# Maxima over partitions by a matmul with the identity instead of POOL's partition operation, with the schedule made anew

## The chip, the cores and the metric

The kernel runs on one core of one Trainium2 chip. Its engines work side by side, each through its own instructions in order: PE multiplies matrices (TensorE) and writes to PSUM; DVE (VectorE), ACT (ScalarE) and POOL (GpSimd) work on elements; SP (SyncE) issues all transfers between memory and the core. The metric is the time of one execution in microseconds, as the device counts it. Its median before the change is 1002.06 us of three runs.

## The reference

Linear attention with random features, and a feed-forward layer over its output.

```python
def phi(x):                                   # x: q or k, scaled by 64 ** -0.25
    proj = np.einsum('bhsd,md->bhsm', x, omega)
    sq = np.sum(x * x, axis=-1, keepdims=True) / 2.0
    h = proj - sq
    h = h - np.max(h, axis=-1, keepdims=True)
    return np.exp(h) / np.sqrt(m)
kv = np.einsum('bhsm,bhsd->bhmd', k_p, v)
z = np.sum(k_p, axis=2)
num = np.einsum('bhsm,bhmd->bhsd', q_p, kv)
den = np.einsum('bhsm,bhm->bhs', q_p, z)[..., None] + 1e-06
x = (num / den)                               # laid out as 4608 tokens x 512
h = x @ w_in                                  # 512 x 2048
out = np.maximum(0.01 * h, h) @ w_out         # 2048 x 512
```

There are 8 batches of 576 tokens, 8 heads of 64, and 128 features. The weights come as 64-bit numbers, which the kernel reads as pairs of 32-bit words. Everything else is float32.

## The kernel before

**Numbers.** Large products are made with pairs of 16-bit numbers, a high part and the rest (`high` and `low_` in the code; three matmuls for each product). To keep the parts in range, omega, the values of each batch and both weights are scaled by a power of two that comes from their largest magnitude. That largest magnitude is first a maximum per partition (`mx_om`, `mx_v0` to `mx_v7`, `mx_w1`, `mx_w2`: eleven in all) and then a maximum over the 128 partitions. The second step is `power_of_two`, at L315 to L330: POOL's `partition_all_reduce` (L320) leaves the maximum in every partition, and four small DVE steps (L324 to L328) cut it to its exponent and invert it. What waits for them: the split of omega, the scaling of the values (`values`), the scaling of a weight's pieces (`Weight.split`), the rows of scales for the output (L644).

**Tiling.** The feed-forward layer works on nine blocks of 512 tokens. For each block, 16 groups of 12 matmuls (L813) make the hidden layer, ACT applies the leaky step (L820), ACT and POOL split it into two parts (L290, L296), and 16 groups of 12 matmuls (L836) make the output. Attention is made ahead of it, batch by batch for keys (`key_batch`) and block by block for queries (`query_block`), two heads at a time. A unit (`Unit`) loads its rows, takes squares, scales (L490 to L495), makes two parts (L506 or L290 and L296), turns them by a transposing transfer (L508), projects them (L520), and has DVE and ACT make the features (L526 to L537). The first two key batches and the first query block are done in whole float32 (`Whole`, L580 to L590), without those transfers. Sums for keys are L682 and L694 to L696, for queries L758 to L765. Both write 260 columns of one PSUM bank of 512, called "mi", of which there is one.

**Weights.** Each weight comes as eight pieces of 1 MB. A piece is converted (`convert`): ACT takes the high words (L403), DVE shifts and joins the low words (L405, L408), PE sums magnitudes (L416), and the sign is put on in one of two ways: by DVE in one step (L426), or, for pieces named in `SIGN_POOL`, by ACT (L421) and POOL (L423). When all eight are done, the maximum of the sums gives the scale (`scale`), and each piece is scaled and split, in one of two ways chosen by `SPLIT_DVE` (L450 or two ACT steps and L296). `Z_POOL` makes the like choice for the units of the first batches or blocks: a unit below its number is scaled in an ACT step of its own and then split.

**Order.** The instructions of each engine stand in an order that a planner in the file works out beforehand (`Plan.order`). Every step has a cost, the buffers it reads and writes, a priority, and sometimes a slack. The planner gives each free engine the step that is ready by its own times. While feed-forward groups are there to fill PE, a step with a slack counts as ready only `SLACK["PE"]` times that slack later; projections and sums of attention have a slack of 1. `PACE` and `LATER` shift the priorities of weights, keys and queries. `PRICE` weighs an engine's time where a step may go to either of two: `high` to ACT or DVE, `low_` to POOL or DVE. The step at L320 is entered as POOL, 0.6 us, the small steps behind it as DVE, 0.65 us. Transfers stand in SP's own order.

The functions that the diff touches, and what calls them:

Of the kernel before, what the change touches and what calls it, by code (L numbers as in the profile page):

```python
# [13 lines left out]
ALU = mybir.AluOpType  # L14
AX = mybir.AxisListType
PSUM = bass.MemoryType.PSUM

P = 128
# [9 lines left out]


EXP_SHIFT = 10.375  # L30
SIGN_POOL = {"w1": [0, 1, 2, 3, 7], "w2": [2]}
SPLIT_DVE = {"w1": [0, 1, 2, 3, 4, 5], "w2": [0, 1, 4, 5, 7]}
Z_POOL = {"k": 1, "q": 2}
PACE = {"k": 9.5, "q": 9.5, "w1": 10.0, "w1s": 0, "w2": 12.0, "w2s": 22.5}

WHOLE = 2
SLACK = {"PE": 1.5}
LATER = {"w1": 20.0, "w2": -295.0, "k": 15.0, "q": -40.0}
ONE = 2.0 ** 14
KV_DOWN = 2.0 ** -24  # L40
H_DOWN = 2.0 ** -15
# [21 lines left out]
class Plan:  # L63
# [2 lines left out]

    HOP = {"PE": 0.25, "ACT": 0.08, "DVE": 0.08, "POOL": 0.10}

    PRICE = {"PE": 1.0, "ACT": 0.68, "DVE": 17.64, "POOL": 1.0, "SP": 1.0}

    def __init__(self, places):
        self.places, self.ops = places, []
# [39 lines left out]
    def order(self):  # L112
# [40 lines left out]
        while len(done) < len(self.ops):  # L153
# [4 lines left out]
            for o in sorted(open_, key=lambda o: (o.prio, o.number)):  # L158
# [3 lines left out]
                if filler:  # L162
                    t += SLACK["PE"] * o.slack
                e = min(o.ways, key=lambda e: max(free[e] + load[e], t) + self.PRICE[e] * o.ways[e][0])
                if t < free[e] + load[e] + 2.0:
# [52 lines left out]
def act(n, pointers=0):  # L218
    return 0.19 + n / 1190 + 0.09 * pointers
# [19 lines left out]
def performer_ffn(ctx: ExitStack, tc, qT, kT, qn, kn, vn, omT, eye, w_in, w_out, out):  # L239
    nc = tc.nc  # L240
# [28 lines left out]
    tiles = {k: [sb.tile(shape, dt, tag=f"{k}{i}", name=f"{k}_{i}") for i in range(n)]  # L269
             for k, (n, shape, dt) in kinds.items()}  # L270
    for k, (n, size) in banks.items():
        tiles[k] = [ps.tile([P, size], F32, tag=f"{k}{i}", name=f"{k}_{i}") for i in range(n)]
    plan = Plan({k: len(v) for k, v in tiles.items()})
    buf, ways = plan.buf, plan.op

    def op(engine, cost, run, port=False, **of):
        return ways([(engine, cost, run, port or engine == "POOL")], **of)

    def high(n, dst, src, scale=None, psum=False, **of):

        pointer = scale is not None and not isinstance(scale, float)
        value = (lambda: scale()) if pointer else (lambda: scale)

        def dve_run():
            if scale is None:
                nc.vector.tensor_copy(dst(), src())
            else:
                nc.vector.tensor_scalar(dst(), src(), value(), None, op0=ALU.mult)
        return ways([
            ("ACT", act(n, int(pointer)), lambda: nc.scalar.activation(dst(), src(), AF.Copy,  # L290
             scale=1.0 if scale is None else value()), False),
            ("DVE", dve(n) if psum else dve2(n), dve_run, not psum)], **of)
# [6 lines left out]
    def at(b):  # L299
        return tiles[b.kind][b.place]  # L300
# [11 lines left out]
    ident = one("ident", [P, P])  # L312


    def power_of_two(mx, name, prio):  # L315


        t = one(f"pow_{name}", [P, 4])
        key = f"pow_{name}"
        op("POOL", 0.6, lambda: nc.gpsimd.partition_all_reduce(t[:, 2:3], mx, P,  # L320
           reduce_op=bass.bass_isa.ReduceOp.absmax), r=[f"mx_{name}"], w=[key], prio=prio)

        def run():
            nc.vector.tensor_scalar(t[:, 1:2].bitcast(U32), t[:, 2:3].bitcast(U32), 0x7F800000, None,  # L324
                                    op0=ALU.bitwise_and)
            nc.vector.tensor_scalar(t[:, 1:2], t[:, 1:2], 2.0 ** -100, None, op0=ALU.max)
            nc.vector.reciprocal(t[:, 3:4], t[:, 1:2])
            nc.vector.tensor_scalar(t[:, 0:1], t[:, 3:4], ONE, None, op0=ALU.mult)  # L328
        op("DVE", 0.65, run, r=[key], w=[key], prio=prio)
        return t, key  # L330


# [4 lines left out]
    def omega():  # L337
        mx = one("mx_om", [P, 1])
        op("SP", 0.45, lambda: nc.sync.dma_start(out=om32(), in_=omT), w=[(whole, "om")], moved=131072, prio=-0.9)
        op("SP", 0.45, lambda: nc.sync.dma_start(out=ident, in_=eye), w=["ident"], moved=65536)  # L340

        def constants():
            nc.vector.memset(ones, 1.0)
            nc.vector.memset(shift, EXP_SHIFT)
            nc.vector.memset(minus_half(), 0.0)
            for j in range(2):
                nc.vector.memset(minus_half()[64 * j:64 * j + 64, j * M:(j + 1) * M], -0.5 * QK_SCALE ** 2)
        op("DVE", 1.0, constants, w=["ones", (whole, "half")], prio=-0.9)

        def scaled():  # L350
            nc.vector.tensor_scalar(om32(), om32(), QK_SCALE, None, op0=ALU.mult)
            nc.vector.tensor_reduce(mx, om32(), axis=AX.X, op=ALU.max, apply_absolute_value=True)
        op("DVE", 0.8, scaled, w=[(whole, "om"), "mx_om"], prio=-0.9)
        t, key = power_of_two(mx, "om", 0)

        def split():
            nc.vector.tensor_scalar(om_c, t[:, 1:2], OM_DOWN, None, op0=ALU.mult)
            for j in range(2):
                r = slice(64 * j, 64 * j + 64)
                a = om32()[r, j * M:(j + 1) * M]  # L360
                nc.vector.tensor_scalar(om[r, 0, :], a, t[r, 0:1], None, op0=ALU.mult)
                nc.vector.scalar_tensor_tensor(om[r, 1, :], a, t[r, 0:1], om[r, 0, :], op0=ALU.mult,
                                               op1=ALU.subtract)
        op("DVE", 1.3, split, r=[(whole, "om"), key], w=["om", "om_c"], prio=0.005)


    class Weight:
# [26 lines left out]
        def convert(self, i, prio):  # L394
# [17 lines left out]
            def sums():  # L412
# [6 lines left out]
               slack=6.0)  # L419
            if i in SIGN_POOL[self.name]:  # L420
                op("ACT", act(1130), lambda: nc.scalar.activation(at(f), high().bitcast(F32), AF.Sign), r=[b], w=[f],  # L421
# [7 lines left out]
        def scale(self, prio):  # L429
            mx = one(f"mx_{self.name}", [P, 1])  # L430

            def run():

                sums = at(self.sums)[:, self.col0:self.col0 + 64]
                if self.name == "w1":
                    nc.vector.tensor_reduce(self.mxs, sums.rearrange("p (f k) -> p f k", k=4), axis=AX.X, op=ALU.add)
                    nc.vector.tensor_reduce(mx, self.mxs, axis=AX.X, op=ALU.max)
                else:
                    nc.vector.tensor_reduce(mx, sums, axis=AX.X, op=ALU.max)
            op("DVE", 0.4, run, r=[(self.sums, self.name, i) for i in range(8)], w=[f"mx_{self.name}"], prio=prio)  # L440
            self.pow, self.key = power_of_two(mx, self.name, prio)

        def split(self, i, prio):
# [3 lines left out]
            whole = lambda: at(f)  # L447
            if i in SPLIT_DVE[self.name]:
                high(1024, lambda: part(0), whole, lambda: self.pow[:, 0:1], r=[f, self.key], w=[(t, 0)], prio=prio)
# [7 lines left out]
        def part(self, i, j):  # L457
            return at(self.parts[i]).bitcast(F16).rearrange("p (a b) -> p a b", a=2)[:, j]
# [5 lines left out]
    class Unit:  # L464
# [7 lines left out]
        def prepare(self):  # L472
# [26 lines left out]
            zh, zl = lambda: at(z)[:, :2 * nt, :D], lambda: at(z)[:, :2 * nt, D:]  # L499
            if self.i < Z_POOL[self.what]:  # L500
                high(n, heads, heads, up, r=[self.sc], w=[nat], prio=prio)
# [104 lines left out]
    def values(b, prio):  # L606
# [9 lines left out]
        for j in range(2):  # L616
# [3 lines left out]
        op("DVE", 0.17, lambda: nc.vector.tensor_reduce(mx, mx2, axis=AX.X, op=ALU.max),  # L620
           r=[f"mx2_v{b}0", f"mx2_v{b}1"], w=[f"mx_v{b}"], prio=prio)
        t, key = power_of_two(mx, f"v{b}", prio)
        hi = lambda: at(both).bitcast(F16)[:, :, :].rearrange("p a b -> p (a b)")[:, :HP * VT * 2 * E].rearrange(
            "p (g d) -> p g d", d=E)
# [28 lines left out]
    def key_batch(b, prio):  # L653
# [6 lines left out]
        for hp in range(HP):  # L660
            plan.like("k", PACE["k"])
            if b >= WHOLE:
# [55 lines left out]
    def query_block(j, prio):  # L718

        for hp in range(HP):  # L720
            plan.like("q", PACE["q"])
            u = Unit("q", j, hp, prio) if j else Whole("q", j, hp, prio)
# [69 lines left out]
    def in_turn(*of):  # L792

        for _ in zip(*of):
            pass
# [51 lines left out]


    omega()
    wsums = buf("ffn")  # L850
    w1, w2 = Weight(w_in, "w1"), Weight(w_out, "w2")
    in_turn(key_batch(0, 1e-4 * LATER["k"]), query_block(0, 1e-4 * LATER["q"]))
    for w in (w1, w2):
        for i in range(8):
            plan.like(w.name, PACE[w.name])
            w.load(i, 1e-4 * LATER[w.name])
            w.convert(i, 1e-4 * LATER[w.name])
        plan.like()
        w.scale(1e-4 * LATER[w.name])
        for i in range(8):  # L860
            plan.like(w.name + "s", PACE[w.name + "s"])
            w.split(i, 1e-4 * LATER[w.name])
    plan.like()
# [61 lines left out]
```

## Time and profile before

| what | value |
|---|---|
| median of three runs | 1002.06 us (1000.24 to 1005.46) |
| the profiled execution | 999.61 us |
| its span (first to last instruction) | 997.8 us |
| busy: PE, DVE, ACT, POOL | 948.5, 561.5, 518.3, 251.3 us |
| granted clock of PE over the span | 0.979 |
| feed-forward matmuls (L813 and L836) | 383.6 and 384.3 us |
| maxima over partitions (L320) | 11, of 0.41 us each |

The profile shows one execution on the chip. "Busy" counts the time in which an engine worked on data, not the time it waited. "Idle before" a group of instructions is what the engine stood still ahead of them, with what released it behind an arrow; "issue" is time in which the engine waited for nothing that the profile shows. The chain of waits goes back from the last instruction, at each step to what released it.

### The profile page before, as it was taken

The numbers are of one execution on the slowest core, as the hardware profiler recorded it, in microseconds if no ns is written. First come the engines' busy times: TensorE is split into PE (matmuls) and PEld (weight loads), VectorE is DVE, ScalarE is ACT, GpSimd is POOL, SyncE is SP. The second block draws the span as 40 slices with busy tenths as digits, with TensorE's granted clock in tenths as the row PEclk, the third lists the DMA queues.
The fourth block names the chain that finished last, engine by engine and source line by source line (L and its number), as shares of the span: only waits on it lengthen the run. The fifth ranks groups of instructions, "written<-read, shape, count | busy, mean of one in ns | idle before, by whom it ended". The sixth has DMA issues, their size and how long they took to land.

```text
span 997.8 us, 16453 instructions
## 1 busy us (share of the span) xinstructions
PE 948.5 (95%) x6576; PEld 523.3 (52%) x6576; DVE 561.5 (56%) x1103; ACT 518.3 (52%) x738; POOL 251.3 (25%) x247
## 2 busy tenths in 40 slices
PE   3778899899899999999999999999999999999998
PEld 3667655555455555555555555554444444444443
DVE  5597966887888887887888888872110000000000
ACT  4368455856584585666775685566114303402410
POOL 2130233300440253112510441024104302401410
PEclk9799799899999999999999999999999999999999
DMA  9463724366356782675585555660430110000000
GB/s 369 143 214 96 215 60 91 74 165 125 66 107 159 131 160 69 141 160 108 102 175 133 99 107 119 129 115 1 74 75 1 32 32 22 1 22 22 1 8 35
DMA packets 211821, 98.69 MB, mean 99 GB/s; under 512 B 170016, under 2 KB 200480, under 8 KB 210720
## 3 DMA queue, kind: packets, MB, share of 16 engines
q1 hardware_dynamic: 211744, 97.64, 42.4%
q8 instruction: 51, 0.84, 0.4%
q14 instruction: 26, 0.21, 0.1%
HBM read 46.50 MB, written 9.44 MB: 56 GB/s over the span
## 4 chain that ended last, share of the span: by engine, by line
PE 78%; DVE 13%; issue 5%; ACT 2%; DMA 1%; POOL 1%; SPq 0%; DVEq 0%; ACTq 0%
PE ffn L836 34%; PE ffn L813 31%; PE pj L520 4%; PE mi L682 3%; DVE st L526 1%; DVE wt L408 1%; DVE p L534 1%; DVE st L586 1%; PE pj L581 1%; PE pj L580 1%; DVE ph L296 1%; PE mi L758 1%; DVE ph L588 1%; DVE wt L405 1%; PE mi L760 1%
## 5 line engine op out<-in xcount | busy, mean ns | idle before, releaser
L836 PE MATMUL ffn<-wt,big 128*128 128x512 f16 x1728 | 384.3, 380 | 0.0
L813 PE MATMUL ffn<-xt,wt 128*128 128x512 f16 x1728 | 383.6, 380 | 0.0
L813 PEld LDWEIGHTS <-wt 128*128 128x128 f16 x1728 | 166.5, 98 | 193.2 <-issue 1.7
L836 PEld LDWEIGHTS <-big 128*128 128x128 f16 x1728 | 166.1, 98 | 191.8 <-issue 1.4
L296 POOL TENSOR_TENSOR big<-row,big 128x512 f16<-128x512 f32 x144 | 177.0, 1233 | 338.5 <-ACT big L290 291.3
L820 ACT ACTIVATE row<-ffn 128x512 f32<-128x512 f32 x144 | 85.2, 592 | 131.9 <-PE ffn L813 79.1
L296 POOL TENSOR_TENSOR xn<-x,xn 128x512 f16<-128x512 f32 x36 | 44.7, 1242 | 231.0 <-ACT xn L290 148.1
L290 ACT ACTIVATE row<-ffn,s 128x512 f32<-128x512 f32 x36 | 24.6, 684 | 147.3 <-PE ffn L836 147.1
L537 ACT ACTIVATE p<-p,shift 128x1024 f32<-128x1024 f32 x68 | 69.8, 1029 | 47.5 <-DVE p L534 47.4
L290 ACT ACTIVATE big<-row 128x512 f16<-128x512 f32 x144 | 90.1, 626 | 2.8
L526 DVE TENSOR_REDUCE st<-pj 128x8 f32<-128x1024 f32 x68 | 72.4, 1075 | 10.8 <-PE pj L520 10.7
L296 DVE TENSOR_TENSOR ph<-p,ph 128x1024 f16<-128x1024 f32 x56 | 70.5, 1261 | 13.4 <-ACT ph L290 13.0
L534 DVE SCALAR_TENSOR_TENSOR p<-pj,sc,st 128x1024 f32<-128x1024 f32 x68 | 76.4, 1132 | 0.3
L778 DVE TENSOR_TENSOR x<-mi,r 128x256 f32<-128x256 f32 x72 | 30.1, 419 | 63.4 <-POOL xn L296 62.3
L520 PE MATMUL pj<-om,t 128*128 128x128 f16 x944 | 61.7, 219 | 3.8 <-DVE p L534 3.0
L520 PEld LDWEIGHTS <-t 128*128 128x128 f16 x944 | 55.0, 98 | 10.3 <-issue 3.4
L290 ACT ACTIVATE ph<-p 128x1024 f16<-128x1024 f32 x56 | 58.7, 1048 | 0.6
L483 ACT ACTIVATE z<-nat 128x512 f32<-128x512 f32 (+1 forms) x56 | 36.0, 645 | 25.6 <-DMA t<-z 13.4
L506 DVE SCALAR_TENSOR_TENSOR z<-nat,sc,z 128x512 f16<-128x512 f32 (+1 forms) x52 | 45.9, 886 | 4.3 <-ACT z L290 4.1
L775 DVE TENSOR_SCALAR r<-mi 128x4 f32<-128x4 f32 x72 | 11.3, 157 | 62.1 <-PE mi L760 61.9
L290 ACT ACTIVATE z<-nat,sc 128x512 f16<-128x512 f32 (+1 forms) x52 | 38.0, 737 | 12.9 <-DVE sc L493 12.9
L290 ACT ACTIVATE xn<-x 128x512 f16<-128x512 f32 x36 | 22.4, 623 | 42.5 <-DVE x L778 36.3
(107 smaller groups left out, 1010.2 us busy)
## 6 DMA issues: line engine op xcount, KB each, us to landing
v<-vn SPq DMA_DIRECT2D x16, 650.0 KB, 5.7
out<-row SPq DMA_DIRECT2D x36, 256.0 KB, 2.1
big<-w_in SPq DMA_DIRECT2D x8, 1024.0 KB, 7.5
big<-w_out SPq DMA_DIRECT2D x8, 1024.0 KB, 5.3
nat<-qn SPq DMA_DIRECT2D x32, 256.0 KB, 3.2
nat<-kn SPq DMA_DIRECT2D x12, 320.0 KB, 3.5
nat<-kn SPq DMA_DIRECT2D x12, 256.0 KB, 3.4
nat<-kT SPq DMA_DIRECT2D x4, 320.0 KB, 5.6
```

The lines of the kernel that those rows point to most:

```text
L290: ("ACT", act(n, int(pointer)), lambda: nc.scalar.activation(dst(), src(), AF.Copy, scale=1.0 if scale is None else value()), False),
L296: return ways([(e, c, lambda g=g: g.tensor_tensor(dst(), a(), b(), op=ALU.subtract), True) for e, c, g in (("POOL", pool_(n), nc.gpsimd), ...
L483: op("ACT", act(n), lambda: nc.scalar.activation(square(), flat(at(nat)[:, :nt, :]), AF.Square, scale=SQ_SCALE), r=[nat], w=[z], prio=prio)
L506: op("DVE", stt(n) + 0.15, lambda: nc.vector.scalar_tensor_tensor(zl(), heads(), up(), zh(), op0=ALU.mult, op1=ALU.subtract), port=True, r ...
L520: nc.tensor.matmul(pv()[:, g], at(self.t)[:, g0 + g, :], om[:, w, :], start=(w == 0), stop=(w == 1))
L526: op("DVE", dve(n * M), lambda: nc.vector.tensor_reduce(row(0), pv(), axis=AX.X, op=ALU.max), r=[pj], w=[st], prio=prio)
L534: op("DVE", dve(n * M), lambda: nc.vector.scalar_tensor_tensor(p(), pv(), down(), row(2).rearrange("p (g o) -> p g o", o=1).broadcast_to([ ...
L537: op("ACT", act(n * M, 1), lambda: nc.scalar.activation(flat(p()), flat(p()), AF.Exp, bias=shift), w=[p32], r=["ones"], prio=prio)
L778: op("DVE", dve(4 * D), lambda av=av, r=r, x=x, i=i: nc.vector.tensor_tensor(at(x)[:, i * 256:(i + 1) * 256].rearrange("p (g d) -> p g d", ...
L813: nc.tensor.matmul(at(ph), wk[wp][:, c:c + P], xt[:, xp, :], start=(i == 0), stop=(i == 3 * KT - 1))
L820: op("ACT", act(512), lambda ph=ph, g=g: nc.scalar.activation(at(g), at(ph), AF.Prelu, scale=H_DOWN, alpha=0.01), r=[ph], w=[g], prio=top)
L836: nc.tensor.matmul(at(po), part(f, gp)[:, t * P:(t + 1) * P], wf[wp], start=(f == 0 and gp == wp), stop=(f == FT - 1 and gp == 1))
```

## The change

The maximum over partitions goes to PE and DVE. The column of 128 maxima, repeated 128 times, is the stationary operand of a float32 matmul, and the identity matrix the moving one: row after row, the result holds all 128 maxima in each partition. It is written to the last 128 columns of the "mi" bank. DVE takes the maximum of each row, and the four small steps follow as before, in the same entry. The identity's load gets the priority of omega's. The numbers that steer the planner are others: which pieces have their sign put on by POOL (seven of w1 instead of five, four of w2 instead of one), which are split in DVE's one-step way (five of w1 instead of six, seven of w2 instead of five), for which units the input is scaled by itself (keys below 3, queries below 3), the paces, priorities, slack and prices.

```diff
-SIGN_POOL = {"w1": [0, 1, 2, 3, 7], "w2": [2]}
-SPLIT_DVE = {"w1": [0, 1, 2, 3, 4, 5], "w2": [0, 1, 4, 5, 7]}
-Z_POOL = {"k": 1, "q": 2}
-PACE = {"k": 9.5, "q": 9.5, "w1": 10.0, "w1s": 0, "w2": 12.0, "w2s": 22.5}
+SIGN_POOL = {"w1": [0, 1, 2, 3, 4, 5, 7], "w2": [0, 1, 2, 7]}
+SPLIT_DVE = {"w1": [0, 1, 4, 6, 7], "w2": [0, 1, 2, 4, 5, 6, 7]}
+Z_POOL = {"k": 3, "q": 3}
+PACE = {"k": 13.5, "q": 9.5, "w1": 0, "w1s": 4.0, "w2": 5.5, "w2s": 15.0}
...
-SLACK = {"PE": 1.5}
-LATER = {"w1": 20.0, "w2": -295.0, "k": 15.0, "q": -40.0}
+SLACK = {"PE": 0.5}
+LATER = {"w1": 0.0, "w2": -305.0, "k": -25.0, "q": -570.0}
...
-    PRICE = {"PE": 1.0, "ACT": 0.68, "DVE": 17.64, "POOL": 1.0, "SP": 1.0}
+    PRICE = {"PE": 1.0, "ACT": 1.09, "DVE": 12.14, "POOL": 1.0, "SP": 1.0}
...
+    scratch = tiles["mi"][0][:, 384:]
...
-        op("POOL", 0.6, lambda: nc.gpsimd.partition_all_reduce(t[:, 2:3], mx, P,
-           reduce_op=bass.bass_isa.ReduceOp.absmax), r=[f"mx_{name}"], w=[key], prio=prio)
+        op("PE", 0.35, lambda: nc.tensor.matmul(scratch, mx.broadcast_to([P, P]), ident, start=True, stop=True),
+           r=[f"mx_{name}", "ident"], w=["scratch"], prio=prio, slack=1.0)
 
         def run():
+            nc.vector.tensor_reduce(t[:, 2:3], scratch, axis=AX.X, op=ALU.max)
...
-        op("DVE", 0.65, run, r=[key], w=[key], prio=prio)
+        op("DVE", 0.95, run, r=["scratch"], w=[key], prio=prio)
...
-        op("SP", 0.45, lambda: nc.sync.dma_start(out=ident, in_=eye), w=["ident"], moved=65536)
+        op("SP", 0.45, lambda: nc.sync.dma_start(out=ident, in_=eye), w=["ident"], moved=65536, prio=-0.9)
```

## The prediction

> **What bounds the kernel now.** I read the page's totals first, then the busy time by stretches.
>
> ```profile
> span 997.8 us, 16453 instructions
> PE 948.5 (95%) x6576; PEld 523.3 (52%) x6576; DVE 561.5 (56%) x1103; ACT 518.3 (52%) x738; POOL 251.3 (25%) x247
> ...
> 0.00:120.00 120.00, 83.39 (x491) 72.85 (x492) 89.40 (x140) 67.77 (x82) 26.17 (x28) 0.86 0.65 213
> 120.00:200.00 80.00, 75.58 (x492) 43.15 (x491) 59.04 (x100) 51.65 (x71) 25.32 (x26) 0.95 0.37 75
> 200.00:365.00 165.00, 162.40 (x1386) 89.87 (x1385) 138.87 (x287) 105.22 (x152) 41.76 (x45) 1.00 0.63 128
> 365.00:440.00 75.00, 73.09 (x608) 40.34 (x606) 62.77 (x133) 46.70 (x69) 19.09 (x20) 1.00 0.54 118
> 440.00:680.00 240.00, 240.00 (x2058) 133.19 (x2057) 202.53 (x416) 161.60 (x231) 65.75 (x65) 1.00 0.59 121
> 680.00:997.80 317.80, 314.04 (x1553) 143.87 (x1551) 8.89 (x31) 85.33 (x137) 73.16 (x63) 1.00 0.10 25
> ```
>
> In the stretches the columns after the length are busy time of PE, its weight loads, DVE, ACT and POOL, the granted clock, the DMA share and GB/s. PE is idle for 997.8 - 948.5 = 49.3 us: 36.61 before 120 us, 4.42 to 200, 2.60 to 365, 1.91 to 440, none to 680, and 3.76 at the end, where the last block is evicted and stored. The matmuls stay the same but for eleven small ones. So time can only come out of these gaps, or out of the stretch in which the clock is 0.86.
>
> The chain of waits names what makes the gaps (start, length, what):
>
> ```profile
> 3.76 5.06 issue
> 8.81 0.42 POOL pow_om L320
> ...
> 24.92 6.23 issue
> ...
> 46.42 1.93 issue
> ...
> 74.64 3.54 issue
> ...
> 133.30 3.43 issue
> ...
> 168.56 5.70 issue
> ...
> 246.44 1.38 issue
> ...
> 384.20 4.29 issue
> ```
>
> Each of these eight pieces stands right before a POOL L320, as the first does. That operation runs 0.42 us; what precedes it is a code load of POOL:
>
> ```profile
> L320 POOLq MODIFY_POOL_CONFIG  x22: 1/11/15, 1.0 to 531.7; - x22
> ...
> 255.57 2.28 POOL L296 TENSOR_TENSOR big<-row,big 128x512 f16<-128x512 f32 x2 [7.34 <-DVE r L776]
> ...
> DVE pow_v L324 <- POOL pow_v L320: 23.6, 6, 6.7
> DVE pow_w L324 <- POOL pow_w L320: 10.1, 2, 6.1
> DVE pow_om L324 <- POOL pow_om L320: 5.5, 1, 5.5
> ```
>
> There are 22 configuration changes for 11 reductions: one into the reduction and one back, after which the next ordinary POOL work waits again (7.34 us at 255.57). DVE, which works in order, stands for 23.6 + 10.1 + 5.5 = 39.2 us at L324. The written order charges 0.6 us for the operation, so much that is ready lies behind that wait: maxima of projections, their subtraction, the splitting of weights.
>
> **The change, part by part.** The maximum itself. Removed from the chain: 5.06 + 6.23 + 1.93 + 3.54 = 16.76 us before 120, 9.13 before 200 and 5.67 later, with 0.42 for each reduction. Added, eleven times: one fp32 matmul of the identity and one DVE maximum over 128 values. The nearest rows:
>
> ```profile
> L739 PE MATMUL ffn<-ident,ph 128*128 128x128 f32 x32 | 5.1, 311 | 1.2 <-ACT ph L590 1.2
> L739 PEld LDWEIGHTS ffn<-ident,ph 128*128 128x128 f32 x32 | 4.4, 169 | 1.4 <-ACT ph L590 1.4
> L436 DVE TENSOR_REDUCE mxs_w<-ffn 128x16 f32<-128x64 f32 x1 | 0.2, 216 | 0.0
> L352 DVE TENSOR_REDUCE mx_om<-xt 128x1 f32<-128x256 f32 x1 | 0.4, 421 | 0.0
> ```
>
> Weight load 0.17 + matmul 0.31 + a reduction between 0.22 and 0.42 (0.29 in proportion) + two hand-overs, which I estimate together at 0.13: 0.9 us, where the chain had 0.42 and the code load. Upper bound: the matmul falls behind a group of 12 FFN matmuls (2.59 us by the two busy rows, 380 ns each being pipelined ones), giving 3.5. Lower bound 0.77, no hand-over. I take 0.9 in the startup, where no FFN group runs.
>
> Startup: 16.76 + 4 x 0.42 - 4 x 0.9 = 14.8 us. Of the omega piece (5.06) I count half, since at that time the first inputs are still arriving and the next DVE work may be late instead: 12.3. Bounds: 0, if everything else is as late, and 14.8.
>
> 120 to 200: the chain would give 9.13 + 0.84 - 1.8 = 8.2, but PE has FFN work to fill with and only 4.42 us of gaps: I take 3.5 (0 to 4.42). 200 to 440: the chain would give 1.38 + 4.29 + 0.84 - 1.8 = 4.7, the gaps are 4.51. DVE is busy 62.77 of 75 us at 365 to 440, and its other work may be late next: I take 2 (0 to 4.5). The last DVE waits fall where PE has no gap, and give nothing.
>
> Cost on PE: seven of the eleven matmuls fall where PE is full. Each takes between its pipelined share (5.1/32 = 0.16) and 0.48: 0.3, so 2 us. Bounds 1 and, if PE stands at each until the maximum is there, 7 x 3.5 = 24 (the longest such waits below).
>
> The clock. The same kind of work at two places of the chain, and the first FFN matmuls behind it:
>
> ```profile
> 87.42 2.32 PE mi L682 x20
> ...
> 110.53 8.79 PE mi L682 x40
> 119.32 11.61 PE ffn L813 x48
> ```
>
> Forty sums took 8.79 us at 110.53 where 2 x 2.32 = 4.64 is the better rate: 4.15 lost there, after a stretch with gaps. All that the clock can give is 83.39 x 0.14 + 75.58 x 0.05 = 15.5 us; none at the other end. With fewer gaps I take 5, near the one place that shows a price. The Trainium skill, "TensorE: Matmul & The Clock Gate" (Part 1), says that PE drops to half its clock after an idle window of about 3.4 us and needs as long a busy one to come back. By that rule the two long gaps alone would matter and the term would be about 6; the rows above agree with half speed, none shows the threshold.
>
> Signs on POOL: two more pieces of w1 and three of w2 lose the DVE step L426 and take an ACT and a POOL step instead.
>
> ```profile
> L426 DVE SCALAR_TENSOR_TENSOR wt<-wt,wt 128x1024 uint32<-128x1024 uint32 x10 | 12.1, 1216 | 0.0
> L421 ACT ACTIVATE wt<-big 128x1024 f32<-128x1024 f32 x6 | 6.9, 1148 | 7.6 <-DVE wt L405 7.6
> 33.96 1.22 DVE L408 SCALAR_TENSOR_TENSOR wt<-big,wt 128x1024 uint32<-128x1024 uint32 x1
> 40.13 3.27 DVE L408 SCALAR_TENSOR_TENSOR wt<-big,wt 128x1024 uint32<-128x1024 uint32 x1
> 39.49 2.84 POOL L423 TENSOR_TENSOR wt<-wt,wt 128x1024 f32<-128x1024 f32 x1 [6.82 <-ACT edge L590]
> ```
>
> DVE saves 5 x 1.22 = 6.1, but L408 took 3.27 instead of 1.22 while POOL's L423 ran: 5 x 2.05 = 10.3 is lost if each meets such a step. Between -6.1 and +4.2 I take nothing; half of the meetings would cancel it. ACT's 5 x 1.15 = 5.7 hides in its 120 - 67.77 = 52 idle us; without that cover they would stand in the weights' path.
>
> The rest, in its order in the diff.
>
> ```profile
> L290 ACT ACTIVATE nat<-nat,sc 128x512 f32<-128x512 f32 x4 | 2.9, 714 | 4.2 <-DVE sc L493 4.2
> ...
> 13.41 0.37 PE L416 MATMUL ffn<-ones,wt 128*128 128x1 bf16 x8 [13.41 <-DVE wt L408]
> ```
>
> Eight more units scale their input in a step of ACT by itself (0.71, so 5.7 us of ACT, hidden in the same way; at worst all of it in the units' path). One weight piece more is split in DVE's one-step way, a step of DVE for a step of DVE; the identity's load moves to the head of SP's queue, ahead of the weights, 64 KB at the 213 GB/s of that stretch being 0.3 us, plus one issue of 0.45; DVE's lower price can move steps there only where ACT or POOL is far behind. Together: 0, between -1 and +7.
>
> The order made anew has no row. PE's first matmul comes at 13.41 us; if that wait stays, 36.61 - 13.41 = 23.2 us of the startup's gaps are the most that any order can close, 10.9 more than the 12.3 counted. It can also open new ones (second rival). I take 0 for it beside the terms above.
>
> Sum: 12.3 + 3.5 + 2 + 5 - 2 = 20.8; the profiled execution took 999.61 us (span 997.8 and 1.8 around it), so 978.8, rounded 979. That execution lies just under the lowest of the runs shown (1000.24; their median is 1002.06). I don't shift for that; it is inside the range.
>
> **The rivals.** (1) Something else is late in the startup. DVE is busy for 89.40 of 120 us, and the weights, the whole of block 0 and its attention go through it. For it: two of the four startup pieces are already short. Against: the other two aren't covered by anything. Then half of the startup and half of the clock's gain: 12.3/2 + 3.5 + 5/2 - 2 = 10.2, 989.
>
> (2) Slower: PE waits in the middle. The slack that the order leaves ahead of projections and attention sums falls from 1.5 to 0.5 us. PE works in order, so whatever is later than planned then stops the FFN matmuls behind it.
>
> ```profile
> L526 DVE TENSOR_REDUCE st<-pj 128x8 f32<-128x1024 f32 x68 | 72.4, 1075 | 10.8 <-PE pj L520 10.7
> L775 DVE TENSOR_SCALAR r<-mi 128x4 f32<-128x4 f32 x72 | 11.3, 157 | 62.1 <-PE mi L760 61.9
> ...
> PE mi L765 <- DVE x L778: 8.5, 3, 3.8
> PE mi L682 <- DVE x L778: 6.6, 3, 3.5
> ```
>
> There are 68 + 72 = 140 such steps beside the key sums. The point where it decides: a mean wait of 20.8/140 = 0.15 us. At 0.25 us each it costs 35, so 979 + 35 = 1014. For it: a margin that falls by 1.0 us. Against: PE has no gap at all from 440 to 680, and an FFN group of 2.59 us rounds most starts up.
>
> (3) No change: the maximum's matmul writes columns 384 to 511 of the one "mi" bank, which the attention sums use. If accesses to the bank are put in turn, each of the eleven waits for a reader of the sums, and the next sums wait for the maximum. PE's waits for that bank's reader average (8.5 + 6.6)/6 = 2.5 us; 11 x 2.5 = 28 is lost if every one meets a reader, 979 + 28 = 1007; a few will find the bank free, and I take 1003. The Trainium skill, "PSUM — Partial Sum Buffer" (PSUM bank collisions raise a hardware error), asks that accesses of two engines be kept apart by bank and not by address. It speaks against this place; no run here shows the wait yet.
>
> (4) The new order goes further: the clock's 15.5 in place of 5, and the 10.9 us more of the startup's gaps, 979 - 10.5 - 10.9 = 958. For it: DVE is idle for 30.6 of the first 120 us. Against: the first inputs have to be there.
>
> That the change doesn't do what it says, code loads that remain, I give no chance of its own: L320 is the only line with configuration changes, and it goes.
>
> **How the numbers follow.** Forecast 0.60, rival (1) 0.12, (2) 0.10, (3) 0.07, (4) 0.11. The range 960 to 1000 leaves out (2), half of (3) and some of (4), 0.18 together. No change means within 0.5%, 997 to 1007, about what a measurement of this kernel can tell: 0.07; faster is the forecast with (1) and (4), 0.83; slower 0.10.
>
> **What would show it.** Right: no L320 configuration changes; DVE's first step after each maximum within 1.5 us; no "issue" of over 2 us ahead of one; the first FFN matmul at about 119 - 12.3 - 4 = 103 us; PE idle of about 30 us in all; the last DVE-heavy stretch ending some 20 us sooner. Clock over 0.90 in the first 100 us bears out the clock's term. Wrong: PE waits between 200 and 680 that add up to over 10 us (rival 2), PE waits at the new matmul for a reader of "mi" (rival 3), or a startup that has kept its length with other waits in it (rival 1).

## The result, and the profile after

The changed kernel takes 972.81 us (median of four runs, 966.78 to 975.21), the kernel before 1003.22 us beside it (1000.24 to 1005.46). The ratio is 0.969, with a 95% interval of 0.9638 to 0.9742. The forecast was 979 us, within 960 to 1000. The profiled executions are 999.61 us before and 966.78 after, so the terms of the forecast, which add up to 20.8 us, stand against 32.8 us there. Both executions are the shortest of those measured beside them; by the medians the gain is 30.4 us.

The profile page's totals of the changed kernel, and its busy time by the stretches that the prediction showed for the kernel before (PE, weight loads, DVE, ACT, POOL, granted clock, DMA share, GB/s):

```profile
span 965.0 us, 16453 instructions
PE 943.4 (98%) x6598; PEld 520.4 (54%) x6598; DVE 559.9 (58%) x1110; ACT 528.4 (55%) x749; POOL 264.7 (27%) x241
...
0.00:120.00 120.00, 103.01 (x620) 78.34 (x621) 108.57 (x155) 84.86 (x106) 44.62 (x31) 0.90 0.70 225
120.00:200.00 80.00, 80.00 (x607) 48.97 (x607) 63.61 (x136) 58.67 (x78) 21.46 (x24) 1.00 0.47 106
200.00:365.00 165.00, 165.00 (x1421) 92.41 (x1418) 139.22 (x289) 116.10 (x171) 53.77 (x53) 1.00 0.59 125
365.00:440.00 75.00, 75.00 (x637) 42.06 (x636) 63.02 (x148) 46.45 (x66) 16.39 (x22) 1.00 0.62 134
440.00:680.00 240.00, 240.00 (x1954) 130.41 (x1953) 179.68 (x363) 150.42 (x215) 68.61 (x61) 1.00 0.54 108
680.00:965.00 285.00, 280.39 (x1371) 128.22 (x1369) 5.81 (x23) 71.87 (x116) 59.90 (x52) 1.00 0.08 23
```

PE has no gap any more from 120 to 680 us, where it had 8.93 us. Before 120 us it is idle for 16.99 instead of 36.61 us, and DVE is busy for 108.57 instead of 89.40. The gaps fall from 49.3 to 21.6 us, and PE's busy time falls by 5.1 although there are 22 more matmul records.

The first feed-forward matmul of the changed kernel, a piece of its chain of waits, and PE's waits over the whole span:

```profile
88.59 2.10 PE L816 MATMUL ffn<-xt,wt 128*128 128x512 f16 x9
...
89.42 4.69 DMA xt<-xn
94.11 0.04 issue
94.15 4.85 PE ffn L816 x15
...
PE mi L322 <- DVE mx_om L355: 3.7, 1, 3.7
PE ffn L816 <- DMA xt<-xn: 3.5, 1, 3.5
PE mi L768 <- DVE x L781: 3.0, 4, 1.4
```

The first feed-forward matmul comes at 88.6 us and not at 119.1. Nine are done, then PE waits 3.5 us for a transfer of turned tokens and goes on at 94.15. L322 is the new matmul. It waits 3.7 us once, for omega at the very start, where PE has nothing else, and practically nowhere later.

The groups of the new operations, and the first weight's maximum in order of time, on DVE and PE:

```profile
L322 PE MATMUL mi<-ident,mx_v 128*128 128x128 f32 x16 | 3.4, 297 | 0.5 <-DVE mx_v L623 0.5
L326 DVE TENSOR_REDUCE pow_v<-mi 128x1 f32<-128x128 f32 x8 | 2.2, 280 | 0.3 <-PE mi L322 0.3
...
51.53 0.17 DVE L440 TENSOR_REDUCE mx_w<-mxs_w 128x1 f32<-128x16 f32 x1
52.36 0.44 PE L322 MATMUL mi<-ident,mx_w 128*128 128x128 f32 x2
53.13 0.26 DVE L326 TENSOR_REDUCE pow_w<-mi 128x1 f32<-128x128 f32 x1
```

The maximum costs DVE 0.28 us and PE 0.43 us (3.4 us over eight; two records each). From the column of maxima (51.70) to DVE's reduction (53.13) it is 1.43 us, of which DVE spends part on other work, and PE the start on attention sums. For the second weight it is 2.6 us (123.67 to 126.28). The old path had 3.5 us of "issue" at this place alone.

### The profile page after: what moved, and what is told of

The parts are those of the page before. It is cut to its first block, busy times and chain, and to the rows that moved or that the text cites. A ratio compares the mean times of both kernels' runs of the same rounds, so it can differ in the third digit from the quotient of the medians.

```text
span 965.0 us, 16453 instructions
## 1 busy us (share of the span) xinstructions
PE 943.4 (98%) x6598; PEld 520.4 (54%) x6598; DVE 559.9 (58%) x1110; ACT 528.4 (55%) x749; POOL 264.7 (27%) x241
## 4 chain that ended last, share of the span: by engine, by line
PE 91%; DVE 5%; DMA 2%; issue 1%; SPq 0%; POOL 0%; ACT 0%; POOLq 0%; ACTq 0%
PE ffn L839 39%; PE ffn L816 39%; PE pj L523 5%; DMA v<-vn 2%; DVE wt L411 1%; PE mi L761 1%; PE mi L685 1%; PE mi L762 1%; PE mi L763 1%; PE mi L697 1%; PE mi L699 1%; DVE wt L408 1%; PE mi L698 1%; DVE ph L591 1%; PE pj L583 1%; DVE st L589 1%
## 5 line engine op out<-in xcount | busy, mean ns | idle before, releaser
L297 POOL TENSOR_TENSOR big<-row,big 128x512 f16<-128x512 f32 x144 | 182.3, 1267 | 365.2 <-ACT big L291 361.7
L297 DVE TENSOR_TENSOR ph<-p,ph 128x1024 f16<-128x1024 f32 x56 | 73.0, 1308 | 10.8 <-ACT ph L291 10.6
L488 DVE TENSOR_REDUCE sq<-z 128x8 f32<-128x512 f32 (+1 forms) x56 | 39.1, 702 | 6.3 <-ACT z L486 6.2
L291 ACT ACTIVATE z<-nat,sc 128x512 f16<-128x512 f32 (+1 forms) x43 | 31.3, 733 | 19.0 <-DVE sc L496 19.0
```

The costliest lines, as they stand in the source:

```text
L297: return ways([(e, c, lambda g=g: g.tensor_tensor(dst(), a(), b(), op=ALU.subtract), True) for e, c, g in (("POOL", pool_(n), nc.gpsimd), ...
L488: op("DVE", dve(n), lambda: nc.vector.tensor_reduce(at(self.sq)[:, :2 * nt], square().rearrange("p (g d) -> p g d", d=D), axis=AX.X, op=AL ...
```

## Experiments

**The exchange alone, in the old order.** The kernel before, with every engine's order kept as it was: where POOL's reduction stood, the matmul and DVE's maximum are issued. The identity's transfer moves up to right behind omega's.

```diff
-        op("POOL", 0.6, lambda: nc.gpsimd.partition_all_reduce(t[:, 2:3], mx, P, ...
+        op("POOL", 0.6, lambda: nc.tensor.matmul(scratch, mx.broadcast_to([P, P]), ident, start=True, stop=True),
...
+            nc.vector.tensor_reduce(t[:, 2:3], scratch, axis=AX.X, op=ALU.max)
```

> The kernel before with the exchange alone, every engine's order left as it was: in place of each POOL reduction stand the matmul and DVE's maximum at the same place of the order, and the identity is loaded right behind omega. Theory A (the code loads on the chain are most of the gain): the terms of the prediction without the new order, 999.6 - 21, so 975 to 985, first feed-forward matmul at about 103 us instead of 119. Theory B (the order made anew carries the gain, other work is late in the old one): 990 to 1000, startup nearly as long, with DVE waits at other lines.

Measured: 969.23 us, ratio 0.967 (0.9647 to 0.9693). Theory A holds, and the gain is larger than it said. The first feed-forward matmul comes at 101.74 us. The order made anew isn't needed for the gain. DVE still waits for the maximum in this order, for the matmul now, but for 12.6 us in all and at most 2.5 us at once, where it was 39.2.

**The exchange with the planner's old numbers.** Here the order is planned anew for the new operation, with the numbers of before.

```diff
-SLACK = {"PE": 0.5}
+SLACK = {"PE": 1.5}
... (and SIGN_POOL, SPLIT_DVE, Z_POOL, PACE, LATER, PRICE as before)
```

> The changed kernel with all the planner's numbers of before (where signs and splits go, paces, priorities, slack, prices): the exchange, with an order planned anew for it, but not with the new numbers. Theory A: 975 to 985, since planning with a true price adds a few us at most to the exchange. Theory B: 985 to 1000, and only the new numbers bring the rest of the way to 973.

Measured: 987.4 us, ratio 0.9841 (0.9813 to 0.9868). Theory A's number is missed: an order planned with the new operation's own price and engine didn't add to the exchange, it lost 18 us of it. PE's busy row of the first stretch in this kernel, and its longest wait:

```profile
0.00:120.00 120.00, 82.36 (x516) 69.03 (x517) 104.16 (x163) 71.25 (x85) 22.42 (x20) 0.87 0.63 219
...
PE ffn L419 <- DVE wt L411: 17.4, 7, 5.9
```

The loss is all in the startup: PE is idle for 37.6 of 120 us there, 17.4 of them for DVE's conversion of weights, and full from 120 to 440 us. With the old numbers, planning anew gives a worse order than the old one kept as it was.

**POOL's reduction in the new order.** The changed kernel, each engine's order kept, with POOL's reduction at the place of each matmul.

```diff
-        op("PE", 0.35, lambda: nc.tensor.matmul(scratch, mx.broadcast_to([P, P]), ident, start=True, stop=True),
+        op("PE", 0.35, lambda: nc.gpsimd.partition_all_reduce(t[:, 2:3], mx, P, ...
...
-            nc.vector.tensor_reduce(t[:, 2:3], scratch, axis=AX.X, op=ALU.max)
```

> The changed kernel in its own order on every engine, with POOL's reduction put back at the place of each matmul. Theory A: the code loads return to the chain, each about 6 us and the way back about 7, so the time goes up by 20 to 45, to 993 to 1018. Theory B: the new order leaves other work in between and loses less than 10: under 983.

Measured: 1006.22 us, ratio 1.0022 (1.0003 to 1.0042) to the kernel before. So the exchange is worth some 34 us in either order, and with POOL's reduction the new order by itself gains nothing.

**The planner told the true price.** The kernel before, with POOL's reduction.

```diff
-        op("POOL", 0.6, lambda: nc.gpsimd.partition_all_reduce(t[:, 2:3], mx, P, ...
+        op("POOL", 7.0, lambda: nc.gpsimd.partition_all_reduce(t[:, 2:3], mx, P, ...
+        op("POOL", 6.5, lambda: None, r=[key], prio=prio)
```

> The kernel before, with POOL's reduction, but the planner is told 7.0 us for it instead of 0.6 and another 6.5 us of POOL behind it. If the harm of the code load is mainly that DVE is sent to wait for it by a wrong price (work that is ready lies behind the wait), DVE's waits at L324 fall from 39 to under 15 us and the time to 985 to 993. If it is the length of the path itself (nothing else is there to do), the time stays within 997 to 1007.

Measured: 1016.72 us, ratio 1.0133 (1.0106 to 1.0159). Both expectations fail. DVE's waits for the reduction are gone from the list of waits altogether, and the time is longer all the same. Another wait leads PE's list:

```profile
PE pj L581 <- DMA nat<-kT: 15.8, 1, 15.8
```

The plan put the first keys' transfer behind others: it is issued at 4.04 us, where it was 2.11. Taking the wrong price away changed the whole order, so this run says nothing on how much the wrong price did; that was asked of the next runs, which keep the order.

**The exchange alone beside the changed kernel, on one chip.**

> The exchange alone in the old order once more, beside the changed kernel on one chip. Theory: what was gained is the exchange's; the order made anew neither adds nor takes away, so the two lie within 4 us of each other, at 968 to 975. Rival: the new order is worth at least 5 us more or less in a direct comparison.

> The changed kernel itself, for the comparison with the exchange alone: within 4 us of it by the theory, 5 us or more apart by the rival.

Measured: 970.16 us (ratio 0.9661, 0.9644 to 0.9679) and 970.42 us (0.9658, 0.9633 to 0.9682). They are equal, as the theory said. No version tried here beats the changed kernel by more than can be told. The first two stretches of the exchange alone; from 200 to 440 us PE is full in it too:

```profile
0.00:120.00 120.00, 98.94 (x616) 79.54 (x617) 98.23 (x163) 76.78 (x96) 29.25 (x34) 0.90 0.67 221
120.00:200.00 80.00, 80.00 (x588) 46.19 (x587) 67.06 (x132) 57.12 (x76) 21.58 (x17) 1.00 0.55 118
```

**POOL's reductions left in, unread.** The exchange in the old order, and POOL still does its eleven reductions at their places.

```diff
+        spare = one(f"spare_{name}", [P, 1])
         op("POOL", 0.6, lambda: (nc.tensor.matmul(scratch, mx.broadcast_to([P, P]), ident, ...),
+           nc.gpsimd.partition_all_reduce(spare, mx, P, ...)),
```

> The exchange in the old order, and POOL still does each of the eleven reductions at its old place, into a column that nobody reads: the code loads are there, but DVE waits for none of them. Theory (the wait of DVE is what counts, POOL's own time is covered): at most 6 us above the exchange alone, so 969 to 976. Rival (POOL is late with its own work, since each load and the way back block it for some 13 us): more than half of the gain is lost, 985 or more.

Measured: 990.81 us, ratio 0.9861 (0.9836 to 0.9887): 20.6 us above the exchange alone, though no one reads the result. The theory falls and the rival holds. The chain of waits of this run shows one way:

```profile
108.51 12.29 PE ffn L815 x48
...
166.16 3.99 issue
170.15 1.16 POOL big L296
171.34 0.60 ACT row L822
171.93 0.95 ACT wt L290
172.91 1.73 DVE wt L296
...
177.03 6.42 PE ffn L838 x29
```

POOL's splitting of the hidden layer (L296) stands behind the way back from the reduction. A row buffer comes free only when it ends, ACT waits for that buffer, and behind it on ACT stand the second weight's pieces, for which PE waits. ACT's waits of that kind, in the kernel before, in this run and in the exchange alone:

```profile
ACT row L820 <- POOL big L296: 52.4, 31, 6.0
```

```profile
ACT row L822 <- POOL big L296: 60.4, 32, 5.7
```

```profile
ACT row L820 <- POOL big L296: 31.9, 24, 1.3
```

The longest falls from 6.0 to 1.3 us only where the loads are gone. PE's stretches of this run say where the 20.6 us lie:

```profile
0.00:120.00 120.00, 97.00 (x542) 78.87 (x543) 95.73 (x153) 72.58 (x90) 27.00 (x31) 0.86 0.67 221
120.00:200.00 80.00, 77.39 (x573) 45.36 (x572) 60.11 (x116) 54.88 (x73) 24.08 (x25) 1.00 0.40 81
200.00:365.00 165.00, 160.50 (x1343) 89.61 (x1342) 136.44 (x282) 105.83 (x157) 45.49 (x47) 0.99 0.61 130
365.00:440.00 75.00, 73.16 (x629) 41.17 (x627) 62.99 (x137) 45.61 (x65) 15.70 (x19) 1.00 0.58 128
```

From 120 to 440 us PE is idle for 8.95 us, as much as in the kernel before (8.93), though DVE waits for no reduction here; in the exchange alone it is nothing. Before 120 us it is idle for 23.0 us, near the 21.1 of the exchange alone and far from the 36.6 before. So the gaps in the middle stay as long as the loads are on POOL, and most of the startup's close as soon as DVE no longer waits. The rest of the loads' price is in PE's busy time, 8.7 us more than in the exchange alone. The first feed-forward matmul in the chain is 8 us later than there (108.51 us; 100.75 in the run on the same chip). Only 2 us of that are gaps; the others are busy time of the 497 matmul records ahead of it, 85.5 instead of 79.7 us, at a granted clock of 0.86 instead of 0.90.

**DVE held, without loads.** The exchange in the old order; ahead of each maximum DVE reduces the identity four times, and nobody reads that.

```diff
+            for _ in range(4):
+                nc.vector.tensor_reduce(idle, ident.rearrange("p (o m) -> p o m", o=1).broadcast_to([P, 8, M]), ...
             nc.vector.tensor_reduce(t[:, 2:3], scratch, axis=AX.X, op=ALU.max)
```

> The exchange in the old order, no code loads, and DVE is held ahead of each of the eleven maxima by four reductions of the identity (about 4.5 us, near the mean wait of before, 39.2 us over nine waits) whose results nobody reads. Theory after the run with the unread reductions (POOL's own lateness is about 20 us of the gain, DVE's wait the other 14): about 985, at most 990. Rival (either alone costs most of it, since both lie on one chain): 994 or more.

Measured: 1013.39 us, ratio 1.0099 (1.0063 to 1.0134). The time is the rival's, 43 us above the exchange alone, but the run doesn't show that the rival is right, since it holds more than DVE. What DVE was held for, by its groups, and the startup's row:

```profile
L326 DVE TENSOR_REDUCE idle_v<-ident 128x8 f32<-128x1024 f32 x32 | 39.0, 1218 | 0.8
L326 DVE TENSOR_REDUCE idle_w<-ident 128x8 f32<-128x1024 f32 x8 | 9.7, 1218 | 0.2
L326 DVE TENSOR_REDUCE idle_om<-ident 128x8 f32<-128x1024 f32 x4 | 4.9, 1217 | 0.1
...
0.00:120.00 120.00, 86.94 (x502) 75.33 (x503) 106.50 (x162) 67.54 (x82) 22.73 (x24) 0.85 0.62 213
```

DVE was held for 53.6 us, more than the 39.2 of its waits before the change. And PE stood behind the held DVE in a way that the kernel before doesn't have: the matmul has written its rows to the "mi" bank, DVE reads them only behind its four reductions, and the attention sums, which use that bank, wait for the reading:

```profile
PE mi L761 <- DVE pow_v L327: 10.7, 3, 4.4
...
PE mi L768 <- DVE pow_w L327: 3.6, 1, 3.6
PE mi L761 <- DVE pow_w L327: 3.4, 1, 3.4
...
PE mi L685 <- DVE pow_v L327: 2.7, 1, 2.7
```

These are 20.4 us, where the exchange alone has 1.2. At the whole rate of 43 us for 53.6, DVE's 39.2 us of before would make 31 us, and without the 19.2 us more of these waits some 18 us (estimates from these figures, the second of them by time alone, without what the waits did to the clock). So the run leaves open what DVE's wait costs by itself: both the theory and the rival lie in that span.

**Both.** POOL's unread reductions and the held DVE stand in one kernel.

> Both together: POOL's unread reductions and DVE held for about 4.5 us at each maximum. If these two are all that the old operation cost, the time is that of the kernel before, 998 to 1010. If it stays under 995, something else of the exchange brings the rest.

Measured: 1016.51 us, ratio 1.0127 (1.0097 to 1.0158), above the range given, since DVE is held here for 53.6 us and not for 39.2. With DVE held the loads add 3 us, without it 20.6, so the two prices don't add up. But here too PE waits 20.4 us for the bank, so the run doesn't say what the two delays of the old operation share. What is measured in one order of taking away: without DVE's waits, but with the loads, the time falls by 14.6 us (1005.4 to 990.81), and without the loads as well by another 20.6.

**Four maxima of eleven.** The exchange in the old order for omega, the values of batches 0 and 1 and the first weight.

```diff
+        mm = name in ("om", "v0", "v1", "w1")
+        op("POOL", 0.6, lambda: (nc.tensor.matmul(...) if mm else nc.gpsimd.partition_all_reduce(...)),
```

> The exchange in the old order for omega, the values of batches 0 and 1 and the first weight alone; the other seven maxima stay with POOL. Theory, by the terms of the prediction: the startup's 12 to 16 us and the clock's 4 to 5 are gained, the 9 us of the later gaps are not: 980 to 985. Rival: the shorter startup only moves PE's wait to the second weight's maximum, so that less than half of the gain is there: 988 or more.

Measured: 982.96 us, ratio 0.9784 (0.9764 to 0.9804), within the theory's range. The startup's four give 22 us, the other seven 13. Two later stretches of this run show that the gaps behind those seven stay as they were before (PE 75.58 and 73.09 there):

```profile
120.00:200.00 80.00, 76.10 (x512) 42.94 (x510) 61.26 (x120) 54.84 (x73) 23.28 (x24) 0.96 0.42 88
...
365.00:440.00 75.00, 72.98 (x615) 40.58 (x612) 63.19 (x138) 45.23 (x64) 12.38 (x17) 1.00 0.67 137
```

**All but omega.** Omega's maximum alone stays with POOL.

```diff
+        mm = name != "om"
```

> The exchange in the old order for all but omega, which stays with POOL. The prediction counted half of omega's 5 us, since other first inputs may be late: 972 to 974 against 970 of the whole exchange. If all of it was on the chain: 975 or more. If the first transfers hide it: 970 to 971.

Measured: 973.59 us, ratio 0.9699 (0.9673 to 0.9725), against 0.9661 (0.9644 to 0.9679) of the whole exchange. The two ran on different chips, and their intervals overlap a little. The difference in the middle is 3 to 4 us, above the half that was counted; neither nearly nothing nor all five can be ruled out.

**The old slack in the changed kernel.**

```diff
-SLACK = {"PE": 0.5}
+SLACK = {"PE": 1.5}
```

> The changed kernel with the old slack of 1.5 instead of 0.5 for projections and sums of attention, planned anew. The second rival (less slack makes PE wait in the middle) would make this faster than the changed kernel, by 5 us or more: under 966. If the small slack costs nothing, 968 to 980, and any loss shows as a longer startup or as PE gaps that the order itself leaves.

Measured: 981.19 us, ratio 0.9779 (0.9751 to 0.9807), some 11 us slower than the changed kernel and just above the range given. No harm of the small slack shows: this run is the one that has PE gaps in the middle, 8.49 us of them in one stretch where the changed kernel has none:

```profile
200.00:365.00 165.00, 156.51 (x1380) 88.95 (x1378) 136.25 (x283) 111.50 (x160) 47.14 (x49) 0.97 0.61 129
```

As the whole order is another, the run doesn't show which of its steps a larger slack put too late.

## Why the prediction was right, point by point

Direction, bound and place were right: PE's gaps, first of all the startup's, were what could be gained, and the reduction with its code loads made them. The size was too small by a third. By the prediction's own terms, against the profiled executions of the run with the reductions left in unread (span 988.0 us), of the exchange alone (the second, 968.4 us) and of the changed kernel:

| term | predicted | loads left in, unread | exchange alone | changed kernel |
|---|---|---|---|---|
| startup's gaps, to 120 us | 12.3 | 13.6 | 15.6 | 19.6 |
| gaps from 120 to 200 us | 3.5 | 1.8 | 4.4 | 4.4 |
| gaps from 200 to 440 us | 2 | -1.8 | 4.5 | 4.5 |
| gaps from 440 to 680 us | 0 | -0.4 | -0.4 | 0 |
| clock, less the new matmuls (PE's busy time) | 5 - 2 = 3 | -3.3 | 5.4 | 5.1 |
| the last stretch | 0 | -0.1 | 0 | -0.9 |
| sum | 20.8 | 9.8 | 29.4 | 32.8 |

The profiled execution of the kernel before, which all three are taken from, is its quickest; by the medians on one chip the three gains are 14.6, 35.2 and 35.0 us.

**The price of the exchange** lies within the bounds given, but above what was taken. 0.9 us were said for weight load, matmul, reduction and hand-overs; it is 0.43 us on PE and 0.28 us on DVE, and 1.4 us from the column to the start of the reduction in the first case shown, 2.6 us for the second weight, where the matmul stands behind other work of PE. So the sign "DVE's first step after each maximum within 1.5 us" isn't borne out for all of them. The first feed-forward matmul, said for about 103 us, comes at 101.74 in the exchange alone. PE's eleven matmuls are busy for 4.8 to 5.1 us, and the eight behind 120 us of the changed kernel for 3.3, where 2 was said for seven.

**The step that was mis-sized is the discount**: "other work may be late next", "DVE ... its other work may be late next", in the startup and in the later gaps. The terms were 3.5 and 2 where the gaps were 4.42 and 4.51, and both closed completely. Nothing else came to be late. The prediction reckoned all gaps by DVE's chain. The load and the way back from it, after which POOL's ordinary work waits, are named there and have no term: they were read as a sign of that same wait. They were a delay beside it: between the third column and the fourth, their removal brings 19.6 of the 29.4 us. With DVE's waits gone and the loads left in, the startup's gaps give 13.6 us, near the 12.3 forecast, and the gaps from 120 to 440 us together give nothing. They close only when the loads are gone too. So the startup's term was right in its cause and nearly in its size. The 5.5 us for the later gaps rested on a wait that doesn't make them by itself, and came in by luck, because the exchange takes both away at once. The startup's bound of 14.8 us, made from DVE's chain alone, is passed in the exchange alone for the same reason: the last 2 of its 15.6 us come with the loads' removal. This holds for one order of taking away. The other, loads gone and DVE still late, was measured only with the bank held as well.

The order planned anew closes 4 us more of the startup's gaps. The profiled executions keep 3.4 us of that in the sum, but the changed kernel's is its quickest, and by the medians of the runs side by side nothing is left.

**Half for omega** agrees with the times as far as they can tell: 3 to 4 us of 5.06, 2.5 counted.

**The clock's term** was too small and in the wrong place. PE's busy time fell by 5.1 us with 5.1 us of new matmuls in it, so the clock gave between 5 and 10 where 5 was said, if nothing else made the matmuls shorter. With the loads left in unread, PE's busy time is 3.3 us above the kernel before, new matmuls included, so most of this gain, too, came with the loads' removal. The granted clock of the two halves of the first 200 us (the number behind POOL's column), before and after:

```profile
0.00:100.00 100.00, 68.30 (x390) 59.09 (x391) 71.48 (x110) 56.90 (x69) 19.93 (x25) 0.90 0.60 205
100.00:200.00 100.00, 90.68 (x593) 56.91 (x592) 76.96 (x130) 62.52 (x85) 31.55 (x29) 0.90 0.47 110
```

```profile
0.00:100.00 100.00, 83.01 (x495) 68.29 (x496) 89.90 (x135) 71.47 (x87) 33.05 (x24) 0.88 0.78 260
100.00:200.00 100.00, 100.00 (x734) 59.02 (x732) 82.29 (x156) 72.06 (x98) 33.02 (x32) 1.00 0.44 94
```

"Over 0.90 in the first 100 us" is not borne out: it is 0.88, against 0.90 before. All that the clock gave came after 100 us, where PE has no gap left and runs at 1.00; 90.68 us of busy time at 0.90 would be some 9 us slow before the change (an estimate).

**Signs on POOL, the units' extra ACT step, splits, prices, the identity's place**: counted at nothing together with the order, and together they are nothing, since the exchange alone and the changed kernel take the same time. Singly they weren't measured: what they give or cost can't be taken out of an order that is planned for them all. What the order made anew does is to undo a harm: with the old numbers the planner, once it knows the new operation, loses 18 us.

**The rivals.** (1), half the startup, falls: its gaps gave 15.6 us and more, and the four early maxima alone bring 22 us. (2), waits in the middle by the small slack, falls: PE has no gap from 120 to 680 us, and the larger slack is slower. (3), turns at the "mi" bank: in the changed kernel's list of PE's waits the new matmul stands behind the maxima themselves, never behind a reader of the sums. One reading of sums by DVE stands behind a new matmul:

```profile
DVE r L778 <- PE mi L322: 2.2, 1, 2.2
```

The Trainium skill's rule on keeping two engines' accesses apart by bank (PSUM — Partial Sum Buffer, PSUM bank collisions raise a hardware error) has little to cost here: 2.2 us of DVE's waits in the changed kernel, and 1.2 us of PE's in the exchange alone. What the rival feared for the next sums is there as soon as DVE is late, as the 20.4 us with DVE held show. No run shows what breaking the rule would do. (4) named too deep a gain: 10.9 us beyond the 12.3 of the startup, where 7.3 were found in the changed kernel and 3.3 in the exchange alone, and 15.5 for the clock, which gave 10 at most.

## What to carry to other kernels

An operation that brings its own code can cost an in-order engine twice, on the way in and on the way back, and what stands behind it on that engine is late even if the result isn't wanted; count both, with what waits for buffers behind them. When an operation brings two delays, take away one and look at each stretch again: a gap that stays is not made by the one taken away alone, whatever the chain of waits named there. A run that adds a delay on purpose must be read for what else it holds, here a bank that others need. And an order tuned by numbers for one set of prices must be compared with itself kept as it is, before a new order is given any credit.

## What was not expected of the hardware

POOL's eleven reductions, with nobody reading them, cost 20.6 us of 970, though POOL is busy for only a quarter of the span, and nearly half of it shows as longer busy time of PE (951.9 against 943.1 us, at a granted clock of 0.981 against 0.988 over the span). DVE held for 53.6 us at the eleven maxima cost 43 us at the end, though in the exchange alone DVE is busy for only 57% of the span; PE spent 20.4 us there waiting for the bank.
